# Linear attention with a SoLU block: three small sums by token placed later, and one transposition of queries done in two halves

## The chip, the cores and the metric

The kernel runs on one core of a Trainium2 chip. A core has five engines that run side by side, each with its own queue, in order: TensorE (PE; its weight loads are shown apart as PEld), VectorE (DVE), ScalarE (ACT), GpSimd (POOL) and SyncE (SP, which here issues DMAs). They wait for each other through semaphores. The metric is the time of one execution on the device in microseconds (us); the lower the better.

## What is computed

Attention with a recurrent state, then a feed-forward block on its output:

```python
for t in range(S):                                   # B, H, S, D = 4, 8, 768, 48
    state = alpha[:, :, t, :, None] * state + k[:, :, t] (outer) v[:, :, t]
    y[:, :, t] = q[:, :, t] @ state
x = y.transpose(0, 2, 1, 3).reshape(B * S, H * D)    # 3072 x 384
h = x @ w_in                                         # 3072 x 1024
e = exp(h - max(h)); solu = h * e / sum(e)
ln = (solu - mean) / sqrt(var + 1e-6) * g_ln
out = ln @ w_out                                     # 3072 x 384
```

## The kernel before

**Groups and chunks.** The sequence is cut into G = 6 groups of P = 128 tokens. A group holds the 128 tokens of all B = 4 batches, so there are 24 chunks of 128 tokens, numbered `n = g * 4 + b`. Queries, keys and alphas lie with 32 partitions for each batch. The head dimension of 48 is split in a first part of 32 (the "firsts", 8 heads of 32 x 128) and a last part of 16 (the "lasts", two heads in one block, 4 blocks).

**One group of attention.** Alpha is transposed (`alpha_T`, L179 and L182 on DVE), scanned backwards and forwards (`scan_back`, `scan_on`, L204 on DVE) into running products; keys and queries are multiplied by these. `lasts(qn, qe)` and `firsts(qn, qv)` are DVE transpositions in blocks of 32 x 32 (L182 and L179); `queries(2)` then multiplies the lasts, `queries(0)` the first four heads of the firsts and `queries(1)` the other four, each one POOL instruction of 128 x 512 (L253). `apart` (L245, two ACT instructions) spreads the lasts over the even and the odd heads. `move_lasts` (8 DMAs) and `move_firsts` (4 DMAs) copy the queries into `lot` for the reading of the state. `scores(a, half)` (L278 on PE) does four heads of the scores: first with the firsts of heads 0, 2, 1, 3, then with the lasts of the even heads and of the odd heads, for all four batches, into the PSUM banks a0 to a3. `masked(half)` (L289 on DVE) takes them out under the causal mask. `read_state` and `read_values` (L333) give y, and `next_state` (L371) the state of the next group.

**One group of the feed-forward block.** For each of the eight slices f of 128 features, `up` computes h (L394 on PE), e = exp(h) (L408 on ACT), u = h * e (L409 on DVE) and the square of u (L412 on ACT). `running` adds up e on POOL and the squares on DVE (both L427) over the slices. `token_sums` reduces these sums over the partitions with PE (L462), transposes the result on DVE (L467) and makes from it, for each token, `s`, the part of the variance that is independent of the mean (L469, L471, L473: three DVE instructions of 128 x 4 or 128 x 8). `down` multiplies by w_out (L507 on PE), whose extra column gives the sum of u, and `finish(n)` makes mean and variance from it (L532 to L537 on DVE, which reads `s`), takes the power -1/2 on POOL (L546), scales on ACT (L548) and stores.

**The order.** The program is written under a manual schedule: the order of the calls in the source is the order in each engine's queue. Waits between engines are put in from the reads and writes of regions of a tile. The first groups are written out by hand (to L845 or so): group 0 alone, then `token_sums(0)`, the preparation of group 1's attention beside the `down` of group 0, then `scores(1, 0)`, `masked(0)`, `alpha_T(2)`, `scores(1, 1)`, `masked(1)`, `finish(0)`, `finish(1)`, `finish(2)`. The group 0 sums' `token_sums(0)` stands ahead of `alpha_T(1)`; its result is first read in `finish(0)`.

From then on a loop over g runs the feed-forward of group g and the attention of group g + 1 together. In slice s of group g it issues in turn: what the plan has at "head", `up(g, s)`, a `finish`, `token_sums(g - 1)` at s = 0, what the plan has "behind", the `centre` steps in group 1, `running(g, s)`, what stands in the "middle", a `down`, and the "tail". For g = 1 the plan is

```python
first = dict(
    head={3: "keys_back"},
    behind={0: "v", 1: "on1", 2: "lasts firsts", 3: "apart", 4: "scores0 masked0", ...},
```

so `attend(2, "lasts")` and `attend(2, "firsts")` stand behind slice 2, ahead of `running(1, 2)`; `apart` behind slice 3, after that slice's square on ACT; and the first scores of the third group (a = 2) behind slice 4. For g = 2 to 4 the plan `usual` has "lasts firsts" at slice 2 too, for a = 3 to 5.

Of the kernel before, what the change touches and what calls it, by code (L numbers as in the profile page):

```python
# [9 lines left out]
FP = mybir.dt.float32  # L10
# [4 lines left out]
ALU = mybir.AluOpType  # L15
AX = mybir.AxisListType
P = 128
# [15 lines left out]
def fast_path(ctx, tc, q, k, v, alpha, moe_w_in, moe_w_out, moe_g_ln, out):  # L33
# [12 lines left out]
    nc = tc.nc  # L46
    B, H, S, D = q.shape
    NTOK, DM = out.shape
    DFF = moe_w_in.shape[1]
    G = S // P  # L50
    N = B * G
    NP = H // 2
# [9 lines left out]
    def pool(name, bufs, **kw):  # L62
        return ctx.enter_context(tc.tile_pool(name=name, bufs=bufs, **kw))
# [4 lines left out]
    small = pool("small", 4)  # L68
# [31 lines left out]
    qn = const.tile([P, H, TQ, D], FP, name="qn")  # L100
# [20 lines left out]
    qv = const.tile([P, 2 * H, SW], FP, name="qv")  # L121
# [6 lines left out]
    gr = [dict() for _ in range(G)]  # L128
# [44 lines left out]
    def load_v(g):  # L173
        t = slice(g * P, (g + 1) * P)
        for b in range(B):
            nc.sync.dma_start(out=held(vn, b), in_=v[b, :, t, :].rearrange("h p d -> p h d"))

    def firsts(src, dst):
        nc.vector.transpose(out=dst.rearrange("p h (t u) -> p h u t", u=TQ), in_=src[:, :, :, 0:E0])  # L179
# [31 lines left out]
    def inverses(g):  # L211
        nc.gpsimd.tensor_copy(out=fend[:, g], in_=h4[:, :, 1])  # L212
        nc.vector.reciprocal(out=seed[:, :, 0:1], in_=h4[:, :, 1:2])
# [5 lines left out]
    def keys_T(g):  # L219
        firsts(kn, kT[:, 0:H])  # L220
        lasts(kn, kT[:, H:NB])

    def keys(g):
        for part in (slice(0, H), slice(H, NB)):
            nc.gpsimd.tensor_tensor(out=kT[:, part], in0=kT[:, part], in1=hk[:, part], op=ALU.mult)  # L225
# [24 lines left out]
    def queries(i):  # L250
        part = slice(NP * i, NP * i + NP)
        q = qe[:, :, 0:P] if i == 2 else qv[:, part, 0:P]
        nc.gpsimd.tensor_tensor(out=q, in0=q, in1=aT[:, part, 1:SW], op=ALU.mult)  # L253
# [11 lines left out]
    def quarter(b):  # L265
        return slice(32 * b, 32 * b + 32)
# [4 lines left out]
    def scores(g, half, a=None):  # L271
        a = a or banks("a", [NP, P])
        for last in range(2):
            for i in (0, 2, 1, 3):
                h = half * NP + i
                kb, qb = (H + h // 2, H + h) if last else (h, h)
                for b in range(B):
                    nc.tensor.matmul(  # L278
                        a[b][:, i], lhsT=kT[quarter(b), kb], rhs=qv[quarter(b), qb, 0:P], start=not last and not i, stop=bool(last),
                        tile_position=(32 * b, 0), skip_group_check=True,  # L280
                    )
        masks[half] = a
# [3 lines left out]
    def masked(half, batches=range(B)):  # L286
        a = masks[half]
        for b in batches:
            nc.vector.tensor_tensor(  # L289
                out=sT[:, b, half * NP : half * NP + NP], in0=a[b], in1=mask[:, None, :].to_broadcast([P, NP, P]),  # L290
                op=ALU.mult,
            )
# [46 lines left out]
    def read_begin():  # L339
        reading["y"] = {}  # L340
        reading["begun"] = set()
# [112 lines left out]
    def token_sums(g):  # L454


        d = gr[g]
        t = ps_a.tile([P, B, 2, 32], FP, tag="a3", name="rows") if g else ps_h.tile([P, B, 2, 32], FP, tag="h", name="rows")
        for b in range(B):
            for r in range(4):  # L460
                c = b * P + 32 * r
                nc.tensor.matmul(  # L462
                    t[quarter(r), b], lhsT=d["unit"][:, 0:32], rhs=d["p"][:, :, c : c + 32], start=True, stop=True,
                    tile_position=(0, 32 * r), skip_group_check=True,
                )
        tt = work.tile([P, B, 2, 32], FP, name="cols")
        nc.vector.transpose(out=tt.rearrange("p b i t -> p (b i t)"), in_=t.rearrange("p b i t -> p (b i t)"))  # L467
        s = sums[:, g * B : g * B + B]
        nc.vector.tensor_copy(out=s[:, :, 1:3], in_=tt[:, :, :, 0])  # L469
        sq = small.tile([P, B], FP, name="sq")  # L470
        nc.vector.tensor_tensor(out=sq, in0=s[:, :, 1], in1=s[:, :, 1], op=ALU.mult)  # L471
        d["s"] = small.tile([P, B], FP, name="s")
        nc.vector.scalar_tensor_tensor(  # L473
            out=d["s"], in0=sq, scalar=1e-6 * DFF, in1=s[:, :, 2], op0=ALU.mult, op1=ALU.add
        )

    def last_norm():

# [39 lines left out]
    def finish(n):  # L518
        g, b = divmod(n, B)
        d = st[n]  # L520
        s, whole = sums[:, n], d.get("held", d["o"])
        o = whole[:, 0:DM]
        t0 = b * S + g * P
        if g == G - 1:
            o_sb = work.tile([P, DM], FP, name="o_sb")
            r = gr[g]["r"][:, b : b + 1]
            nc.vector.tensor_scalar(out=o_sb[:, 0:P], in0=o[:, 0:P], scalar1=r, scalar2=None, op0=ALU.mult)  # L527
            nc.scalar.activation(out=o_sb[:, P:DM], in_=o[:, P:DM], func=AF.Copy, scale=r)  # L528
            nc.scalar.dma_start(out=out[t0 : t0 + P, :], in_=o_sb)
            d.clear()  # L530
            return
        nc.vector.tensor_copy(out=s[:, 0:1], in_=whole[:, DM : DM + 1])  # L532
        t = small.tile([P, 1], FP, name="t")
        nc.vector.scalar_tensor_tensor(
            out=t, in0=s[:, 0:1], scalar=-1.0 / DFF, in1=s[:, 0:1], op0=ALU.mult, op1=ALU.mult
        )
        nc.vector.tensor_tensor(out=s[:, 3:4], in0=t, in1=gr[g]["s"][:, b : b + 1], op=ALU.add)  # L537
        if g == 0:

            centred = work.tile([P, DM], FP, name="o_mean")  # L540
            nc.vector.scalar_tensor_tensor(
                out=centred, in0=mean_sb, scalar=s[:, 0:1], in1=o, op0=ALU.mult, op1=ALU.add
            )
            o = centred
        r = small.tile([P, 1], FP, name="r")
        nc.gpsimd.tensor_tensor(out=r, in0=s[:, 3:4], in1=mhalf, op=ALU.pow)  # L546
        o_sb = work.tile([P, DM], FP, name="o_sb")
        nc.scalar.activation(out=o_sb, in_=o, func=AF.Copy, scale=r)  # L548
        nc.sync.dma_start(out=out[t0 : t0 + P, :], in_=o_sb)
        d.clear()  # L550
# [166 lines left out]
    for i in (0, 2, 1):  # L717
        if i == 1:
# [3 lines left out]
            out=qe[:, :, 0:P] if i == 2 else qv[:, part, 0:P], in0=t[i], in1=aT[:, part, 1:SW], op=ALU.mult  # L722
# [98 lines left out]
    down(2, 1)  # L821
    scores(1, 1)
    masked(1)
    finish(0)
    finish(1)
    finish(2)
# [36 lines left out]
    def attend(a, what):  # L863

        more = a + 1 < G
        if what == "v":
            load_v(a)
        elif what == "keys":
            keys_T(a)
            keys(a)  # L870
            if more:
                load(k, kn, a + 1)
        elif what[:2] == "on":
            if what == "on2":
                inverses(a)
            scan_on(a, int(what[2]))
        elif what == "lasts":
            lasts(qn, qe[:, :, 0:P])
            ends_of_decay()
            queries(2)  # L880
            move_lasts()
        elif what == "firsts":
            firsts(qn, qv[:, 0:H, 0:P])
            queries(0)
            queries(1)
            move_firsts()
            if more:
                load(q, qn, a + 1)
        elif what == "apart":
            apart()  # L890
        elif what == "decay":
            decay(a)
        elif what == "keys_back":
            if more:
                keys_back(a)
        elif what[:6] == "scores":
            scores(a, int(what[6]))
        elif what[:6] == "masked":
            masked(int(what[6]))
        elif what == "alpha" and more:  # L900
            alpha_T(a + 1)
            if a > 2:
                attend(a, "over")
        elif what == "over" and more:
            alpha_over(a + 1)
            if a + 2 < G:
                load(alpha, an, a + 2)
        elif what == "back" and more:
            for i in range(3):
                scan_back(a + 1, i)  # L910
        elif what == "begin":
            read_begin()
        elif what[:4] == "read":
            read_state(int(what[4]))
        elif what == "values":
            read_values(a)
        elif what == "kv" and more and a != 4:
            next_state(a)
# [3 lines left out]
    for g in range(1, G + 1):  # L922
# [10 lines left out]
        for s in range(FC):  # L933
# [18 lines left out]
            if todo:  # L952
                n, half = todo.pop(0)
# [24 lines left out]
    def compare(out, x, bound, op):  # L978
# [6 lines left out]
        out=chunks[:, :, 2], in0=sums[:, :, 2], scalar=0.25, in1=sums[:, :, 3], op0=ALU.mult, op1=ALU.is_le  # L985
# [6 lines left out]
    else:  # L992
# [9 lines left out]
        out=bad, in0=all_ok[0:1, 0:1], scalar1=float(P * ends[-1]), scalar2=None, op0=ALU.is_lt  # L1002
# [451 lines left out]
```

## Time and profile before

| | us |
|---|---|
| median of 3 runs (368.16 to 368.46) | 368.23 |
| the profiled execution, on the device | 367.97 |
| its span, first to last instruction | 366.2 |
| PE busy | 357.8 (98%) |
| PE weight loads busy | 215.0 (59%) |
| DVE busy | 245.0 (67%) |
| ACT busy | 146.4 (40%) |
| POOL busy | 132.2 (36%) |

The granted TensorE clock is 1.000 over the span. A profile is of one execution; times in it run from its first instruction. A timeline row gives start, length, engine, line, operation, output<-inputs by the program's names, shapes, the number of instructions merged, and in brackets the engine's idle time before it with the instruction that ended it. Ends of matmuls are modelled, since they are pipelined; start times are not. Neighbouring rows of DVE may overlap by about 0.1 us[...].

### The profile page before, as it was taken

Reading aid. Unit: us, or ns where it says so; the run is one execution under the profiler, and the core shown is the slowest. Engines: PE = TensorE matmul, PEld = TensorE weight load, DVE = VectorE, ACT = ScalarE, POOL = GpSimd, SP = SyncE. Lnnn points to the kernel's source line nnn. Section 1 sums busy time; section 2 is a strip of 40 time slices with the busy share of each in tenths; the row PEclk is TensorE's granted clock in tenths of the full one; section 3 lists DMA queues with packets and bytes.
Section 4 is the critical chain, followed back from the end, with each engine's and each line's share of the span. In section 5 each row is a group of like instructions: output and inputs, shape, how many; then the busy total and the mean of one; then the engine's idle time right before and its main releaser. Section 6 shows DMA issues by size and latency. Waiting matters only on the chain. (4 is left out here: it accounts for less than half of the span.)

```text
span 366.2 us, 10036 instructions
## 1 busy us (share of the span) xinstructions
PE 357.8 (98%) x4341; PEld 215.0 (59%) x4341; DVE 245.0 (67%) x375; ACT 146.4 (40%) x260; POOL 132.2 (36%) x129
## 2 busy tenths in 40 slices
PE   8899999999999999999999999999999999999994
PEld 8784355666755566566575456475556565555552
DVE  0999989979998797936675935766946314345420
ACT  3647878182645262252521252431241132222110
POOL 7020000004449963774133764232773121233300
PEclk9999999999999999999999999999999999999999
DMA  9995995326196409463035354004041000000011
GB/s 180 183 338 152 204 309 124 88 67 159 50 234 141 109 21 180 85 152 94 21 92 112 83 121 126 3 25 88 21 107 55 0 25 0 24 21 22 23 47 51
DMA packets 72871, 36.06 MB, mean 98 GB/s; under 512 B 48232, under 2 KB 70000, under 8 KB 72816
## 3 DMA queue, kind: packets, MB, share of 16 engines
q1 hardware_dynamic: 71792, 34.39, 39.8%
q10 hardware_dynamic: 1024, 0.92, 0.8%
q8 instruction: 36, 0.59, 0.7%
q14 instruction: 19, 0.16, 0.2%
HBM read 25.30 MB, written 4.72 MB: 82 GB/s over the span
## 5 line engine op out<-in xcount | busy, mean ns | idle before, releaser
L507 PE MATMUL o<-w_out,room 128*128 128x385 f32 x384 | 134.0, 492 | 0.0
L394 PE MATMUL h<-x,w_in 128*128 128x512 f32 x288 | 131.7, 597 | 0.5 <-DVE g_col L642 0.5
L507 PEld LDWEIGHTS o<-w_out,room 128*128 128x128 f32 x384 | 71.0, 189 | 54.7 <-issue 13.1
L394 PEld LDWEIGHTS h<-x,w_in 128*128 128x128 f32 x288 | 53.2, 189 | 58.6 <-issue 48.5
L409 DVE TENSOR_TENSOR room<-h,e 128x512 f32<-128x512 f32 x40 | 27.5, 689 | 72.9 <-ACT e L408 72.9
L408 ACT ACTIVATE e<-h 128x512 f32<-128x512 f32 x40 | 24.0, 599 | 100.2 <-PE h L394 100.2
L427 POOL TENSOR_TENSOR p<-p,e 128x512 f32<-128x512 f32 x30 | 43.7, 1458 | 20.0 <-ACT e L408 19.9
L412 ACT ACTIVATE u<-room 128x512 f32<-128x512 f32 x40 | 25.2, 630 | 38.3 <-DVE room L409 38.3
L546 POOL TENSOR_TENSOR r<-sums,mhalf 128x1 f32<-128x1 f32 x20 | 14.8, 741 | 69.7 <-DVE sums L537 69.4
L289 DVE TENSOR_TENSOR sT<-a,mask 128x512 f32<-128x512 f32 x43 | 26.7, 681 | 8.0 <-PE a L278 7.9
L204 DVE TENSOR_TENSOR_SCAN hT<-aT,unit 128x516 f32<-128x516 f32 x18 | 24.4, 1399 | 7.6 <-ACT aT L703 7.5
L204 DVE TENSOR_TENSOR_SCAN aT<-aT,seed 128x516 f32<-128x516 f32 x18 | 27.4, 1551 | 0.2
L225 POOL TENSOR_TENSOR kT<-kT,hT 128x1024 f32<-128x1024 f32 (+1 forms) x8 | 14.2, 1800 | 32.7 <-DVE kT L179 32.7
L427 DVE TENSOR_TENSOR p<-p,u 128x512 f32<-128x512 f32 x30 | 22.5, 749 | 5.1 <-ACT u L412 5.1
L278 PEld LDWEIGHTS a<-qv,kT 32*128 32x128 f32 x704 | 21.4, 186 | 7.0 <-issue 2.6
L278 PE MATMUL a<-qv,kT 32*128 32x128 f32 x704 | 23.9, 278 | 0.4 <-POOL qv L253 0.3
L212 POOL COPY fend<-hT 128x12 f32<-128x12 f32 x6 | 3.1, 509 | 55.9 <-DVE hT L204 55.9
L333 PE MATMUL y<-sT,vn 128*32 128x128 f32 x768 | 22.6, 273 | 0.2 <-DVE sT L289 0.2
L333 PEld LDWEIGHTS y<-sT,vn 128*32 128x32 f32 x768 | 20.7, 110 | 1.6 <-issue 1.0
L196 ACT ACTIVATE sq<-an,mone 128x1536 uint8<-128x1536 f32 x12 | 18.9, 1572 | 0.2
L548 ACT ACTIVATE o_sb<-o,r 128x384 f32<-128x384 f32 x16 | 9.3, 582 | 18.5 <-POOL r L546 18.5
L261 POOL TENSOR_TENSOR state<-state,lot 128x384 f32<-128x384 f32 x10 | 8.8, 903 | 13.1 <-DMA lot<-qv 13.1
(148 smaller groups left out, 374.3 us busy)
## 6 DMA issues: line engine op xcount, KB each, us to landing
vn<-in_v_dram SPq DMA_DIRECT2D x24, 192.0 KB, 4.7
an<-in_alpha_dram SPq DMA_DIRECT2D x20, 192.0 KB, 4.1
out_dram<-o_sb SPq DMA_DIRECT2D x20, 192.0 KB, 1.9
room<-in_moe_w_out_dram SPq DMA_DIRECT2D x8, 384.0 KB, 5.5
kn<-in_k_dram SPq DMA_DIRECT2D x16, 192.0 KB, 5.6
qn<-in_q_dram SPq DMA_DIRECT2D x16, 192.0 KB, 4.1
lot<-qe SPq DMA_DIRECT2D x40, 64.5 KB, 2.1
lot<-qv SPq DMA_DIRECT2D x20, 129.0 KB, 2.4
```

Of the source, the lines that this page charges most:

```text
L196: nc.scalar.activation(out=sq, in_=x, func=AF.Relu, scale=sign, bias=mone, accum_out=over[:, g, i : i + 1])
L204: nc.vector.tensor_tensor_scan(out=o, data0=a, data1=s, initial=1.0, op0=ALU.mult, op1=ALU.add)
L278: nc.tensor.matmul(a[b][:, i], lhsT=kT[quarter(b), kb], rhs=qv[quarter(b), qb, 0:P], start=not last and not i, stop=bool(last), tile_posit ...
L289: nc.vector.tensor_tensor(out=sT[:, b, half * NP : half * NP + NP], in0=a[b], in1=mask[:, None, :].to_broadcast([P, NP, P]), op=ALU.mult,)
L333: nc.tensor.matmul(y_bank(b)[quarter(r), a], lhsT=lhsT, rhs=rhs, start=(b, r) not in begun, stop=stop, tile_position=(row, 32 * r), skip_g ...
L394: nc.tensor.matmul(h, lhsT=w_in[:, a, f * P : (f + 1) * P], rhs=d["x"][:, a].rearrange("p b t -> p (b t)"), start=(a == 0), stop=(a == KC ...
L408: nc.scalar.activation(out=e, in_=h, func=AF.Exp)
L409: nc.vector.tensor_tensor(out=u, in0=h, in1=e, op=ALU.mult)
L412: nc.scalar.activation(out=u2, in_=u, func=AF.Square)
L427: eng.tensor_tensor(out=p, in0=d[0][i] if f == 1 else p, in1=d[f][i], op=ALU.add)
L507: nc.tensor.matmul(d["o"][:, 0 : DM + 1], lhsT=u_of(g, f)[:, b * P : b * P + P], rhs=w_out[:, f], start=(f == 0), stop=(f == FC - 1), skip ...
L546: nc.gpsimd.tensor_tensor(out=r, in0=s[:, 3:4], in1=mhalf, op=ALU.pow)
```

## The change

Two edits. In `token_sums` the three DVE instructions behind the transposition L467 become an inner function: for g > 0 it is called where they stood, for g = 0 it is kept and called ahead of `finish(0)`, after `masked(1)`. In `attend`, for a = 2, the transposition of the firsts is done in two parts of four heads, with the POOL product of each part issued after it; for other a it stays whole (`for j in range(0, 2)` then issues the same two products as before). NP is 4, H is 8.

```diff
         tt = work.tile([P, B, 2, 32], FP, name="cols")
         nc.vector.transpose(out=tt.rearrange("p b i t -> p (b i t)"), in_=t.rearrange("p b i t -> p (b i t)"))
         s = sums[:, g * B : g * B + B]
-        nc.vector.tensor_copy(out=s[:, :, 1:3], in_=tt[:, :, :, 0])
-        sq = small.tile([P, B], FP, name="sq")
-        nc.vector.tensor_tensor(out=sq, in0=s[:, :, 1], in1=s[:, :, 1], op=ALU.mult)
-        d["s"] = small.tile([P, B], FP, name="s")
-        nc.vector.scalar_tensor_tensor(
-            out=d["s"], in0=sq, scalar=1e-6 * DFF, in1=s[:, :, 2], op0=ALU.mult, op1=ALU.add
-        )
+        def rest():
+            nc.vector.tensor_copy(out=s[:, :, 1:3], in_=tt[:, :, :, 0])
+            sq = small.tile([P, B], FP, name="sq")
+            nc.vector.tensor_tensor(out=sq, in0=s[:, :, 1], in1=s[:, :, 1], op=ALU.mult)
+            d["s"] = small.tile([P, B], FP, name="s")
+            nc.vector.scalar_tensor_tensor(
+                out=d["s"], in0=sq, scalar=1e-6 * DFF, in1=s[:, :, 2], op0=ALU.mult, op1=ALU.add
+            )
+
+        if g:
+            rest()
+        else:
+            d["rest"] = rest
...
     scores(1, 1)
     masked(1)
+    gr[0]["rest"]()
     finish(0)
     finish(1)
     finish(2)
...
         elif what == "firsts":
-            firsts(qn, qv[:, 0:H, 0:P])
-            queries(0)
-            queries(1)
+            for i, n in ((0, NP), (NP, NP)) if a == 2 else ((0, H),):
+                firsts(qn[:, i : i + n], qv[:, i : i + n, 0:P])
+                for j in range(i // NP, (i + n) // NP):
+                    queries(j)
             move_firsts()
             if more:
                 load(q, qn, a + 1)
```

## The prediction

> **What bounds the kernel now.** I first read the busy shares on the page: TensorE (PE) is busy for 357.8 of the 366.2 us span, VectorE (DVE) for 245.0, ScalarE (ACT) 146.4, GpSimd (POOL) 132.2. The chain that ended last holds only the final output tile, so it says nothing about the middle. Since PE is nearly always busy, an edit on another engine can move the end only where PE waits for that engine. So I asked next for PE's waits between 58 and 135 us, where both edits lie. Columns: who waited, for whom, us in total, times, longest.
>
> ```profile
> PEld a L278 <- DVE qv L811: 0.3, 1, 0.3
> PE a L278 <- POOL qv L253: 0.3, 1, 0.3
> ```
>
> Both are scores (L278): one waits for DVE, one for POOL. The ends of matmuls are modelled, so a stall can hide inside a busy block. The PE timeline (start, length, what) shows it, because the same 64 matmuls recur:
>
> ```profile
> 77.87 2.69 PE L278 MATMUL a<-qv,kT 32*128 32x128 f32 x64
> ...
> 83.28 2.07 PE L278 MATMUL a<-qv,kT 32*128 32x128 f32 x64
> ...
> 107.55 5.32 PE L394 MATMUL h<-x,w_in 128*128 128x512 f32 x12
> 113.12 2.26 PE L278 MATMUL a<-qv,kT 32*128 32x128 f32 x64 [0.26 <-POOL qv L253]
> ```
>
> The undisturbed block is 2.07. The first one (group two, half 0) carries 0.62 of stall inside: bank a1 still holds the query block that L811 reads until 78.45. The one at 113.12 (group three, half 0) starts about 0.3 late (0.26 by modelled ends, 0.33 against the start-to-start step before the scores at 118.09) and has 0.19 inside. All of PE's stalls within reach are thus 0.62 + 0.33 + 0.19 = 1.14 us. After the block at 118.09, which is lengthened by 0.14 by the masking before it, equal blocks repeat at equal steps to 345 us: a shift of PE at 120 us is neither absorbed nor enlarged later, unless an engine falls behind.
>
> The DVE timeline next:
>
> ```profile
> 62.69 0.44 DVE L467 STREAM_TRANSPOSE cols<-rows 128x256 f32<-128x256 f32 x1
> 63.16 0.17 DVE L469 COPY sums<-cols 128x8 f32<-128x8 f32 x1
> 63.37 0.17 DVE L471 TENSOR_TENSOR sq<-sums 128x4 f32<-128x4 f32 x1
> 63.57 0.17 DVE L473 SCALAR_TENSOR_TENSOR s<-sq,sums 128x4 f32<-128x4 f32 x1
> 63.65 2.17 DVE L179 STREAM_TRANSPOSE aT<-an 128x1024 f32<-128x1024 f32 x1
> ...
> 109.55 2.05 DVE L179 STREAM_TRANSPOSE qv<-qn 128x1024 f32<-128x1024 f32 x1
> 111.43 0.69 DVE L427 TENSOR_TENSOR p<-p,u 128x512 f32<-128x512 f32 x1
> 112.02 0.69 DVE L409 TENSOR_TENSOR room<-h,e 128x512 f32<-128x512 f32 x1
> ...
> 118.12 1.50 DVE L427 TENSOR_TENSOR p<-p,u 128x512 f32<-128x512 f32 x1
> ```
>
> Here stand the three small sums that move, the transposition that is cut, and behind it the running sum L427 and the product L409. The same running sum takes 0.69 at 111.43 and 1.50 at 118.12. POOL says why:
>
> ```profile
> 109.78 1.09 POOL L253 TENSOR_TENSOR qe<-qe,aT 128x512 f32<-128x512 f32 x1 [1.65 <-DVE qe L182]
> 111.68 2.44 POOL L253 TENSOR_TENSOR qv<-qv,aT 128x512 f32<-128x512 f32 x2 [0.81 <-DVE qv L179]
> ...
> 117.11 1.96 POOL L662 TENSOR_TENSOR w_out<-w_out,mean_sb 128x384 f32<-128x384 f32 x2
> ```
>
> POOL's second L662 started at 118.07 and ended at 119.07; the DVE sum that came at 118.12 ended 0.55 later, at 119.61. It waited for the whole POOL instruction. Last, ACT:
>
> ```profile
> 112.75 0.63 ACT L412 ACTIVATE u<-room 128x512 f32<-128x512 f32 x1 [1.41 <-DVE room L409]
> 113.28 1.32 ACT L245 ACTIVATE qv<-qe,parity 128x512 f32<-128x512 f32 x2
> ```
>
> L245 (`apart`) makes the queries for the second halves of the score matmuls. It stands on ACT behind the square L412, which waits for DVE's L409. The odd heads' copy ends at 114.61 and PE starts their matmuls at 114.66. So this block of scores has two gates: POOL's first product at its start, and DVE -> ACT -> `apart` before its last quarter.
>
> **What the Trainium skill says.** "SBUF — State Buffer", section "Who interferes with whom": a DVE instruction with two SBUF inputs and a GpSimd instruction that reads SBUF exclude each other for the whole instruction, whichever issues first; a DVE instruction with one SBUF input does not contend. The trace agrees: the sum L427 was held at 118.12, while L253 took 1.09 beside the transposition, and L409, whose h lies in PSUM, keeps 0.69 beside POOL. "VectorE: DVE Perf Modes", section "The TRN2 errata — SBUF-src ops pay a fixed extra latency per instruction": small instructions cost mostly a fixed part. Here a 128x4 sum takes 0.17 and a 128x512 one 0.69.
>
> **Part 1, the sums by token.** Removed near 63 us: three instructions. From L467 to the next transposition is 0.97 now; L467 alone holds the engine for 0.3 to 0.4 (0.44 less the overlap of 0.08 to 0.15 seen between independent neighbours). DVE runs 0.6 to 0.65 earlier. It has no gap up to L811 at 77.76, apart from 0.1 ahead of L804, so bank a1 comes free at 77.85 and the 0.62 stall inside the first score block goes: PE gains 0.6. No other wait replaces it, since the matmuls ahead of it do not depend on this DVE work and the transposed keys in kT are ready at 72.5. The loads of alpha (SP at 66.87), `move_lasts` and `move_firsts` (SP at 74.78 and 80.15) come 0.6 earlier too, behind nothing new. The masks at 80.41, which wait for PE, follow by 0.6, and so does everything on DVE up to 88.02.
>
> Added ahead of `finish(0)`: copy to square 0.21, square to sum 0.20, sum to next 0.08, hence 0.49, with no POOL reader beside them. Queued behind: `finish(0..2)`, then `scan_back(2)` and all of DVE's work to 113 us. So from 88 us DVE is 0.6 - 0.49, about 0.12 early (0.05 to 0.2), while PE is 0.6 early. PE needs DVE in between only for the h buffers: L409 ends at 102.84 - 0.12, and the third h block wants its bank at 103.66 - 0.6 = 103.06. That holds. Alone, part 1 gains PE nothing lasting beyond this 0.12, since the scores of group three wait for DVE's descendants.
>
> **Part 2, the firsts in halves.** One 128x1024 transposition (1.88 to the next start) becomes two of 128x512. The nearest row is the lasts, 128x512, 0.96 to the next start at 109.55. Added: 0 to 0.06; below nothing is excluded, as the elements are the same. DVE's second half ends as before. With the 0.12 from part 1 the first half starts at 109.43 and lands at 110.54, POOL's product of the lasts (109.66 to 110.75) hides the wait, and `queries(0)` runs from 110.72 to 111.81 (1.09). Before, it ran from 111.68 to 113.07. PE's scores may start at 113.12 - 0.33 - 0.6 = 112.2 without a wait.
>
> But now DVE's L427 arrives at 111.43 - 0.12 to + 0.06, about 111.34, with `queries(0)` in the middle of its run. Both read two operands in SBUF. It is held to 111.81, and the next instruction, L409, starts 0.47 after POOL's end (119.07 to 119.54 in the example): 112.28 instead of 112.02, +0.26. Behind it in order: the square at 113.00 (0.72 later, as before), `apart` at 113.54 (0.54 later), its odd copy done at 114.86 (1.32 later), PE's odd quarter at 114.91 instead of 114.66. PE has meanwhile waited some 1.2 us in the middle of the block, where it now waits 0.19. So the start gate opens, and the other gate closes 0.25 later. Everything after on PE is 0.25 late.
>
> What else moves: `queries(1)` waits for L427 and ends near 113.45 instead of 114.12. `move_firsts` isn't helped, since SP is still issuing the eight `move_lasts` until 116.1. POOL's running sums come 0.5 to 0.7 earlier, and then meet DVE's L427 at 113.66 and at 118.37. The latter is nearly a tie with POOL's sum at 118.2: if POOL is first, L409 after it slips to 119.96 (0.42 later) and the masks free their last bank at 123.1, just before PE's `read_state` at 123.26. So no further PE loss, with 0.13 to spare; if DVE is first it recovers 0.4. From 127 us DVE idles 1.5 us and is level again.
>
> Sum: +0.25 on the profiled execution's 367.97 (span 366.2 and 1.8 around it), thus 368.2. The median of the runs is 0.26 above the profiled one, so I predict 368.23 + 0.25 = 368.5.
>
> **Rivals.**
> (a) DVE's L427 isn't held, for instance because it needs the port only briefly. Then `apart` keeps the 0.12 of part 1: 368.1. Against: three running sums (113.41, 118.12, 122.57) all end 0.55 after a POOL instruction.
> (b) Slower: POOL keeps the port from `queries(0)` straight into `queries(1)`, and L427 waits for both. Place: 111.8. Price: another 1.09 before L409, so `apart`, PE's odd quarter and the end are 1.3 late: 369.5. It decides if `queries(1)` starts right at 111.8. Against: at 119.03 POOL's next sum took 1.72, 0.45 more than its 1.27, so it let the waiting DVE in first. For it: all these handovers are POOL to DVE at other instructions. The same size would result if the second half's transposition had to wait for `queries(0)` to release `qv`. Against that, PE's first scores started at 113.12 while POOL was still writing the other heads.
> (c) Faster: all 1.14 us of stall go, 367.1. It needs `apart` about 1 us earlier, and nothing in the change moves it by more than 0.12. It would take a DVE start before 109 us that this trace does not show.
>
> **Chances.** Forecast 0.62, (a) 0.14, (b) 0.17, (c) 0.07. Within 0.2% is within 0.74 us, about what a measurement of this kernel can tell from no change. The forecast (0.05 of it beyond the bound, should the tie at 118.4 or the bank at 123.1 go wrong by half a microsecond) and (a) lie inside: same 0.71; slower 0.17 + 0.05 = 0.22; faster 0.07. The forecast's own range is 368.2 to 368.9, by the 0.05 to 0.2 of DVE's lead and that tie; to leave out no more than 2 in 10 the range takes in (a) and the lower part of (b): 367.9 to 369.5.
>
> **What would show it.** Right: the first score block near 77.9 back to about 2.07; L427 near 111.3 taking about 1.0 instead of 0.69; the block of the third group's first scores starting near 112.2 but ending near 115.6, with PE's wait now on ACT's L245. Wrong: an L427 of 0.69 there (a), of over 2 (b), or an `apart` that starts before 113 (c).

## The result, and the profile after

The changed kernel takes 368.62 us (median of 22 runs, 368.33 to 369.65) against 368.15 us for the kernel before (22 runs beside them, 367.66 to 369.10): ratio 1.0014, 95% interval 1.0009 to 1.0020, which is 0.3 to 0.7 us more. The profiled execution took 368.34 us with a span of 366.5, 0.37 us more than that of before.

PE's timeline of the changed kernel, the blocks that answer to those of before:

```profile
77.90 2.07 PE L278 MATMUL a<-qv,kT 32*128 32x128 f32 x64
...
112.19 1.17 PE L278 MATMUL a<-qv,kT 32*128 32x128 f32 x32
114.40 1.34 PE L278 MATMUL a<-qv,kT 32*128 32x128 f32 x32 [1.04 <-ACT qv L245]
```

The first score block has lost its 0.62 us of stall (2.07, the undisturbed length), and PE reaches the third group's first scores at 112.19, 0.93 earlier than before. It does the half of the block that uses the firsts, and then waits: what ends the wait is no longer POOL but ACT's `apart`. The next block starts at 115.67 instead of 115.32. From there to the end the PE blocks start 0.33 to 0.37 later than before, and the profiled execution is 0.37 longer: in the profile the loss is made here.

DVE and POOL of the changed kernel at that place:

```profile
109.55 2.09 DVE L179 STREAM_TRANSPOSE qv<-qn 128x512 f32<-128x512 f32 x2
111.49 0.97 DVE L427 TENSOR_TENSOR p<-p,u 128x512 f32<-128x512 f32 x1
112.39 0.68 DVE L409 TENSOR_TENSOR room<-h,e 128x512 f32<-128x512 f32 x1
...
118.47 1.55 DVE L427 TENSOR_TENSOR p<-p,u 128x512 f32<-128x512 f32 x1
119.95 0.68 DVE L409 TENSOR_TENSOR room<-h,e 128x512 f32<-128x512 f32 x1
```

```profile
109.78 1.09 POOL L253 TENSOR_TENSOR qe<-qe,aT 128x512 f32<-128x512 f32 x1 [1.66 <-DVE qe L182]
110.83 2.58 POOL L253 TENSOR_TENSOR qv<-qv,aT 128x512 f32<-128x512 f32 x2
```

POOL's `queries(0)` now starts at 110.83 instead of 111.68 and ends at 111.92. DVE's running sum L427, which had run ahead of it before, arrives at 111.49 in the middle of it, takes 0.97 instead of 0.69 and ends 0.55 after POOL. L409 behind it starts at 112.39, 0.37 later than before. ACT follows:

```profile
113.11 0.63 ACT L412 ACTIVATE u<-room 128x512 f32<-128x512 f32 x1 [1.76 <-DVE room L409]
113.64 1.32 ACT L245 ACTIVATE qv<-qe,parity 128x512 f32<-128x512 f32 x2
```

The square and `apart` start 0.36 late, and PE's block behind these scores 0.35.

Where the small sums went, on DVE:

```profile
79.98 2.48 DVE L289 TENSOR_TENSOR sT<-a,mask 128x512 f32<-128x512 f32 x4 [2.46 <-PE a L278]
...
87.63 0.14 DVE L470 COPY sums<-cols 128x8 f32<-128x8 f32 x1
87.81 0.17 DVE L472 TENSOR_TENSOR sq<-sums 128x4 f32<-128x4 f32 x1
88.01 0.17 DVE L474 SCALAR_TENSOR_TENSOR s<-sq,sums 128x4 f32<-128x4 f32 x1
88.09 0.15 DVE L538 COPY sums<-lot 128x1 f32<-128x1 f32 x1
```

The masks start at 79.98, 0.43 earlier than before; `finish(0)` starts at 88.09, 0.07 later. By the firsts DVE stands where it stood: 109.55 in both kernels.

### The profile page after: what moved, and what is told of

Read it like the earlier page. It is cut to its first block, busy times and chain, and to the rows that moved or that the text cites. A ratio compares the mean times of both kernels' runs of the same rounds, so it can differ in the third digit from the quotient of the medians.

```text
span 366.5 us, 10037 instructions
## 1 busy us (share of the span) xinstructions
PE 357.7 (98%) x4341; PEld 214.6 (59%) x4341; DVE 245.4 (67%) x376; ACT 146.2 (40%) x260; POOL 130.7 (36%) x129
## 5 line engine op out<-in xcount | busy, mean ns | idle before, releaser
L409 DVE TENSOR_TENSOR room<-h,e 128x512 f32<-128x512 f32 x40 | 27.5, 688 | 72.7 <-ACT e L408 72.7
L427 POOL TENSOR_TENSOR p<-p,e 128x512 f32<-128x512 f32 x30 | 42.1, 1405 | 20.0 <-ACT e L408 19.9
L427 DVE TENSOR_TENSOR p<-p,u 128x512 f32<-128x512 f32 x30 | 23.5, 782 | 5.2 <-ACT u L412 5.2
```

What stands on the lines that cost most here:

```text
L409: nc.vector.tensor_tensor(out=u, in0=h, in1=e, op=ALU.mult)
L427: eng.tensor_tensor(out=p, in0=d[0][i] if f == 1 else p, in1=d[f][i], op=ALU.add)
```

## The experiments

Timed ratios here have intervals of about +-0.1%, or +-0.35 us, as wide as the effects. So the readings rest on distances inside the traces, one profile of each kernel, and the ratios stand beside them. The traces also start differently: PE reaches the sums by token (L462 in the kernel before) at 60.18 us in the profile of before, at 60.21 after, and between 60.18 and 60.84 over all profiles, so the two that are compared above are among the earliest. A distance from one instruction to another is free of that, as long as the two hang together. "Firsts to scores" is the time from the start of the third group's transposition of firsts to the end of its first scores, read as the start of PE's next block, since ends of matmuls are modelled.

| kernel | first scores start | firsts start | firsts to scores | ratio to before (95%) |
|---|---|---|---|---|
| before | 77.87 | 109.55 | 5.77 | |
| after | 77.90 | 109.55 | 6.12 | 1.0014 (1.0009 to 1.0020) |
| e1 sums alone | 77.97 | 109.62 | 5.82 | 1.0012 (1.0001 to 1.0022) |
| e12 e1 again | 78.25 | 109.90 | 5.76 | 1.0005 (0.9996 to 1.0013) |
| e2 halves alone | 78.40 | 109.77 | 6.12 | 1.0001 (0.9993 to 1.0009) |
| e3 other half first | 78.08 | 109.72 | 5.77 | 1.0003 (0.9995 to 1.0012) |
| e4 sum behind product | 78.53 | 110.18 | 5.24 | 1.0006 (0.9993 to 1.0018) |
| e5 before, PE late | 78.31 | 109.53 | 5.75 | 1.0014 (1.0004 to 1.0024) |
| e6 sums alone, PE late | 78.41 | 110.06 | 5.83 | 1.0028 (1.0020 to 1.0035) |
| e7 spread early | 78.00 | 109.64 | 4.89 | 1.0002 (0.9992 to 1.0012) |
| e8 spread early, sums late | 78.23 | 109.96 | 4.77 | 1.0008 (1.0000 to 1.0016) |
| e9 new order | 78.27 | 109.90 | 4.80 | 0.9999 (0.9988 to 1.0010) |
| e10 new order alone | 78.19 | 109.73 | 5.44 | 0.9992 (0.9983 to 1.0001) |
| e11 e5 again | 78.77 | 109.95 | 5.76 | the profiled run alone |

**Each part alone.** My theory was that POOL's earlier product holds up DVE's sum and so `apart` (called "port"). The rivals: that the second transposition itself costs (cut), or that the sums at 88 us make DVE late (moved sums).

```diff
# e1: the whole change without the halves
-            for i, n in ((0, NP), (NP, NP)) if a == 2 else ((0, H),):
+            for i, n in ((0, H),):
# e2: the whole change without the moved sums
-        if g:
-            rest()
-        else:
-            d["rest"] = rest
+        rest()
...
-    gr[0]["rest"]()
```

> Only the three small sums are moved; the firsts are transposed whole. Theory (port): no change of the end, 0 +- 0.1 us against the kernel before. The first score block near 77.9 loses its 0.6 us of stall, PE arrives 0.6 early at the third group's first scores and waits there for POOL's queries(0) until 113.1, so about 0.9 us instead of 0.3; L427 behind the firsts takes 0.69. Rival (moved sums): the sums at 88 us make DVE late for all that follows, and this run alone is 0.3 us or more slower than before. Rival (cut): 0, since nothing is cut.

> Only the firsts of the third group are transposed in halves; the small sums stand where they stood. Theory (port): +0.37 us against before, as with the whole change: L427 near 111.5 takes about 1.0 us, L409 behind it starts at 112.4, and the block of first scores ends at 115.7. The first score block near 77.9 keeps its 0.6 us of stall. Rival (moved sums): 0. Rival (cut, the second transposition itself costs): +0.37 as well, so that this run does not tell it from the port.

The halves alone give the full 6.12 us, with L427 held. DVE of e2:

```profile
111.65 1.04 DVE L427 TENSOR_TENSOR p<-p,u 128x512 f32<-128x512 f32 x1
112.61 0.68 DVE L409 TENSOR_TENSOR room<-h,e 128x512 f32<-128x512 f32 x1
```

The moved sums alone (e1) give 5.82, and 5.76 in the second run of that kernel (e12), as before, with L427 at 0.74 and 0.68: no loss in this stretch. DVE and PE of e1:

```profile
111.50 0.74 DVE L427 TENSOR_TENSOR p<-p,u 128x512 f32<-128x512 f32 x1
```

```profile
113.24 2.26 PE L278 MATMUL a<-qv,kT 32*128 32x128 f32 x64 [0.30 <-POOL qv L253]
```

So the 0.35 that the traces lose in this stretch belongs to the halves. Two expectations missed. In e1 PE waited for POOL only 0.37 us, counted in start times, instead of 0.9: it had already lost 0.61 at 94.7 us in a wait that nothing shown ended, and that came out of the same wait; in e12 it is 0.94. And the timed runs don't order the two parts as the traces do. For e2 the interval is 0.3 us less to 0.3 us more than before, whose upper end only touches the 0.35 of its trace; for e1 it is 0 to 0.8 us more, with no loss in its trace. By the medians of the same runs (e1 368.32, e2 368.29, before 368.09) the two parts cost about the same. So the timed runs by themselves do not say which part makes the loss.

**The cut or the port.** This run keeps both transpositions but swaps them, so that `queries(0)` can't start before L427.

```diff
-            for i, n in ((0, NP), (NP, NP)) if a == 2 else ((0, H),):
+            for i, n in ((NP, NP), (0, NP)) if a == 2 else ((0, H),):
                 firsts(qn[:, i : i + n], qv[:, i : i + n, 0:P])
-                for j in range(i // NP, (i + n) // NP):
-                    queries(j)
+            queries(0)
+            queries(1)
```

> The whole change, but heads 4 to 7 are transposed before heads 0 to 3, and both products come after: as many DVE instructions as in the change, while queries(0) can start only after the second half, when L427 has begun. Theory (port): L427 takes 0.69 to 0.72, L409 starts at 112.0 to 112.1, the end is 0 +- 0.12 us against before, and PE waits for POOL until 113.1 to 113.2. Rival (cut): L409 stays at 112.3 to 112.4 and the end at +0.3. Rival (moved sums): +0.3.

DVE and PE of e3:

```profile
109.72 2.06 DVE L179 STREAM_TRANSPOSE qv<-qn 128x512 f32<-128x512 f32 x2
111.61 0.69 DVE L427 TENSOR_TENSOR p<-p,u 128x512 f32<-128x512 f32 x1
112.20 0.69 DVE L409 TENSOR_TENSOR room<-h,e 128x512 f32<-128x512 f32 x1
```

```profile
113.29 2.27 PE L278 MATMUL a<-qv,kT 32*128 32x128 f32 x64 [0.87 <-POOL qv L253]
```

As many DVE instructions, L427 back at 0.69, firsts to scores 5.77. From the firsts to L409 it is 2.48, as in the kernel before (2.47), against 2.84 with the change. The cut costs nothing that can be seen in this stretch; the loss is in the time at which POOL's product runs. Further on e3 loses 0.21 us that the kernel before doesn't: at `read_state`, from 123.18 to the next block at 124.48, 1.30 instead of 1.10, where PE's weight loads wait for POOL's state product. The kernel before with a late PE (e11, below), which has neither part of the change, loses as much at the same place, so this is not put down to the cut.

**The sum put behind the product.** Here the halves stay, and L427 is taken from in front of L409.

```diff
                 up(g, s)
+                if (g, s) == (1, 3):
+                    later.pop()()
```

`later` holds the call that issues DVE's running sum of slice 2.

> The whole change, but DVE's running sum of slice 2 is issued behind the product L409 of slice 3 instead of ahead of it, so that what POOL holds up isn't ahead of L409. Theory (port): L409 starts at 111.5 instead of 112.39, apart ends near 114.0, the third group's first scores end at 114.8 instead of 115.67; the end is between 0 and 0.2 us below the kernel before, since the second scores then wait for the masks, which stand behind two sums on DVE. Rival (cut, or moved sums): L409 gains no more than the 0.6 us of the sum itself against 112.39, hence 111.8 or later, and the end stays above that of the kernel before.

DVE and PE of e4:

```profile
110.18 2.11 DVE L179 STREAM_TRANSPOSE qv<-qn 128x512 f32<-128x512 f32 x2
112.05 0.77 DVE L409 TENSOR_TENSOR room<-h,e 128x512 f32<-128x512 f32 x1
```

```profile
113.09 2.39 PE L278 MATMUL a<-qv,kT 32*128 32x128 f32 x64
115.42 2.84 PE L394 MATMUL h<-x,w_in 128*128 128x512 f32 x6
118.19 2.80 PE L278 MATMUL a<-qv,kT 32*128 32x128 f32 x64
```

L409 follows the transposition by 1.87 us instead of 2.84, and firsts to scores falls to 5.24. The second scores then take 0.73 longer than the undisturbed 2.07, since they wait for the masks, which stand behind two sums on DVE. They end 10.74 us after the firsts' start, where the change has 11.03 and the kernel before 10.68. So the mechanism stands, and the small gain that I expected at the end didn't come.

**The second gate by itself.** `apart` is put ahead of slice 3's square on ACT (the third argument of `up_act` is called between product and square):

```diff
-        up_act(g, f)
+        up_act(g, f, apart if (g, f) == (1, 3) else None)
...
-            0: "v", 1: "on1", 2: "lasts firsts", 3: "apart", 4: "scores0 masked0", ...
+            0: "v", 1: "on1", 2: "lasts firsts", 4: "scores0 masked0", ...
```

> The whole change, with apart (L245, two ACT instructions) of the third group issued ahead of slice 3's square instead of behind it. L427 is still held. Theory (port, closing gate is apart behind the square): PE has no wait for ACT left, the third group's first scores run from 112.2 to 114.2 (2.0 us), and PE then waits 1 us or more for the masks in the second scores, which end no earlier than 0.1 us below the kernel before; the end is -0.2 to +0.2 us against before. Rival (the gate is another, such as POOL or DVE directly): the first scores still end after 115.

PE of e7:

```profile
112.53 2.07 PE L278 MATMUL a<-qv,kT 32*128 32x128 f32 x64
114.53 2.84 PE L394 MATMUL h<-x,w_in 128*128 128x512 f32 x6
117.30 3.14 PE L278 MATMUL a<-qv,kT 32*128 32x128 f32 x64
```

With L427 still held (1.10), the first scores have no wait: the gate that closed was `apart` behind the square. All of it is given back in the second scores, 3.14 instead of 2.07, which wait for DVE's masks. The second scores end 10.73 us after the firsts' start, against 10.68 before. So in this order PE's earlier arrival is worth nothing at the end, since DVE's masks come next.

**A late PE.** The timed loss is 0.47 us by the medians and the profiles' 0.37, which its interval of 0.3 to 0.7 still holds; but e1, which loses nothing in its trace, measured above 1. With the sums moved there is no wait left inside the first score block, and in the kernel before this wait could swallow a PE that comes late from the start. Two idle matmuls of 128x128 ahead of `down(1, 0)` make PE late at a fixed place:

```diff
+    warm(2, ps_a, "a1")
     down(1, 0)
     scaled(7)
```

> The kernel before, with two idle matmuls of 128x128 on PE ahead of the second chunk's down at 60.8 us; their result is not used. They make PE about 0.5 us late at a place that depends on nothing of DVE. Theory (cushion): in the kernel before such lateness is swallowed by the 0.62 us wait for bank a1 inside the first score block, which shrinks to about 0.1; the firsts of the third group start at the same distance from the alpha transposition at 63.6 as before (45.9 us), and the end is 0 to +0.15 us against before. Rival (no cushion): PE's 0.5 us stay to the end, +0.5.

> The moved sums alone, firsts whole, with the same two idle matmuls on PE. Theory (cushion): with the sums moved there is no wait left inside the first score block, so PE's 0.5 us reach the masks, DVE's sums at 88 us, the firsts and the third group's scores: about +0.5 us against before and +0.5 against the moved sums alone, and the firsts start at about 110.05 instead of 109.6. That would explain why the change measures more than the 0.37 us that its profile shows. Rival (no cushion effect): the end of this run is as that of the kernel before with the same two matmuls.

> The kernel before with two idle matmuls on PE once more, for its profile. In the first look PE's lateness was gone at the third group's scores, and 0.44 us were lost at 142 us in a wait that no semaphore ended. If that belongs to chance, it is not there now and the span from the second scores' end to the scores of the fourth group is 43.45 us as before; if it belongs to the program, it is there again and that distance is 43.9.

> The moved sums alone once more, for a narrower interval. Theory (cushion): a profile that begins as early as that of before shows no loss, but PE's later starts pass through, so the median is 0.1 to 0.3 us above before. Rival: no difference, within 0.1 us.

PE and DVE of e5, the kernel before with PE late:

```profile
78.31 2.07 PE L278 MATMUL a<-qv,kT 32*128 32x128 f32 x64
```

```profile
109.53 2.04 DVE L179 STREAM_TRANSPOSE qv<-qn 128x1024 f32<-128x1024 f32 x1
```

and of e6, the moved sums with PE late:

```profile
78.41 2.07 PE L278 MATMUL a<-qv,kT 32*128 32x128 f32 x64
```

```profile
110.06 2.12 DVE L179 STREAM_TRANSPOSE qv<-qn 128x1024 f32<-128x1024 f32 x1
```

PE is late by 0.44 and 0.54 against before. In e5 the stall in the score block shrinks to nothing and the firsts start on time; in e6 they are late by 0.51. (DVE came to the query block L812, L811 in the kernel before, at 77.44 in e5, 0.32 earlier than before, so that nothing of the stall was left where about 0.1 was expected.)

The two columns of the table say the same without any idle matmuls. In each kernel with moved sums the firsts are late by about what PE was late at the first scores: e12 +0.38 and +0.35, e9 +0.40 and +0.35, e8 +0.36 and +0.41, e4 +0.66 and +0.63. In e2 and e10, where the sums are not moved, PE was late by 0.53 and 0.32, and the firsts by 0.22 and 0.18, which is about what DVE was late at the small sums (63.16 before, 63.41 in e2, 63.35 in e10). In e11 PE was late by 0.90, more than the wait of 0.62 can swallow, and the firsts by 0.40. So the moved sums take away a cushion of up to 0.62 us.

In time, e6 is 0.7 to 1.3 us above before. But e5 is above it as well, by 0.1 to 0.9 us where 0 to 0.15 was expected. By the medians e6 is 0.58 us above e5 (369.27 of 22 runs, 368.69 of 13), while the moved sums without a late PE cost 0.23 (e1) and 0.20 (e12). This points to the cushion and against the rival that e6 ends as e5 does, though the step from 0.2 to 0.58 is about what such medians scatter. The trace of e5 is level with before at 120.2 us and then takes 44.00 us instead of 43.45 to the fourth group's first scores. Of these 0.55 us, 0.44 are lost ahead of 142.02 in a wait that nothing shown ended, and 0.10 in the block that follows. In the second profile of that kernel (e11) this distance is 43.82: 0.21 more for POOL's state at 123.4 us, and at 142 only the 0.10. It has further such waits at 240, 287 and 294 us, 0.76 together with that at 142. So neither of the two answers fits: the wait at 142 is not the program's at its first size, and others took its place. What they are is open.

The cushion is shown in the traces up to 120 us. How much of the timed 0.47 us its loss makes is not settled, since e12 measured +0.2 us with an interval that reaches no change.

**Towards a faster order.** With `apart` ahead of the square, I also moved DVE's running sums of group 1: first those of slices 2 and 3 behind `masked(0)` (e8), then the one of slice 2 behind slice 3's product and those of slices 3 and 4 behind `masked(1)` (e9), and the latter on the kernel before, with neither part of the change (e10).

```diff
+            if i and g == 1 and f in (2, 3, 4):
+                later.append(add)
+            else:
+                add()
...
+                up(g, s)
+                if (g, s) == (1, 3):
+                    later.pop(0)()
...
             at("behind", s)
+            while later and s == 5:
+                later.pop(0)()
```

This is e9's edit beside the one of `apart`, which is as in e7; `add` issues one engine's sum. e8 holds back slices 2 and 3 only, issues both at s == 4, and has nothing at slice 3.

> As the run before, and DVE's running sums of slices 2 and 3 are issued behind masked(0) in slice 4, so that neither stands ahead of L409 or of the masks. Theory (port, and DVE's order is what PE waits for): first scores 112.2 to 114.2, masks from about 114.4, second scores from 117.0 with at most 0.2 us of wait inside; PE is 1.0 to 1.2 us ahead of the kernel before, ratio about 0.997. Rival (PE gains are taken back later by POOL's state or by banks): the lead is below 0.4 us at the end.

> The whole change, with apart of the third group ahead of slice 3's square, DVE's running sum of slice 2 behind the product of slice 3, and those of slices 3 and 4 behind masked(1). Theory: with neither a held sum nor apart in front, the first scores run 112.2 to 114.2 and the second 117.0 to 119.0 without a wait, masked(1) ends by 122.2, and PE reaches read_state at about 121.9; there it waits for POOL's state product, which waits for the last of the DMAs of move_firsts (121.2 us on SP's queue, not moved by any of this), until 122.9. So of 1.1 us won some 0.9 are taken back there: -0.1 to -0.3 us against before. Rival (no such gate): the full 1.1 us stay, ratio about 0.997.

> The kernel before with the three moves of the run above, without the moved small sums and without the halves. Theory: PE arrives at the third group's first scores at 112.8, queries(0) is ready at about the same time, so 0.5 us are won up to 120 us and the state of POOL takes back all but 0.1 of it: -0.1 us against before, and not slower than the run above, since the wait in the first score block that swallows a late PE is kept. Rival (halves or moved sums are needed): no gain ahead of 120 us, PE's first scores still at 113.1.

In all three both score blocks take 2.07 without a wait, here in e10:

```profile
113.18 2.07 PE L278 MATMUL a<-qv,kT 32*128 32x128 f32 x64
...
117.95 2.07 PE L278 MATMUL a<-qv,kT 32*128 32x128 f32 x64
```

e8 measured 1.0008, where about 0.997 was expected. Its gain was lost at `read_state`: three sums stood ahead of `masked(1)`, and PE waited for the banks that it frees (2.54 us to the next block instead of 1.10):

```profile
123.36 1.52 PE L333 MATMUL y<-lot,state 64*32 64x128 f32 x62 [0.69 <-DVE sT L289]
```

In e9 PE waited there for POOL, but for a reason of its own:

```profile
121.27 2.09 POOL L261 TENSOR_TENSOR state<-state,lot 128x384 f32<-128x384 f32 x2 [1.76 <-DMA lot<-qv]
```

Two state products take 1.65 in the kernel before and 2.09 here, and the second of them 1.29 instead of 0.85: DVE's sum at 121.96, which took 0.70, was running when it was issued. It is the same meeting as in the change, with the sides reversed. In e10 the sum comes at 122.43, the products take 1.64, and the expected wait at `read_state` isn't there: PE starts 0.32 later than in the profile of before and is 0.27 ahead of it at the fourth group's scores (163.41 against 163.68). Its median is 368.00 against 368.22 beside it. It is the best of all kernels here, but the interval reaches 1, so that it beats the kernel before is likely and not shown.

## Why the prediction was right

The forecast of 368.5 us, no change that clears 0.2%, stands against 368.62 and +0.14%. The number alone says little: the range of 367.9 to 369.5 us also held no change at all and alternative (a). What decides is the path that the forecast named, which the profile follows: an L427 of about 1.0, first scores that start near 112.2 and end near 115.6, and PE waiting on L245. By its steps:

- **The stall in the first score block goes.** Shown: 2.07, and from the start of L467 to the next transposition's 0.36 instead of 0.96.
- **DVE would be 0.12 early from 88 us on.** This term was wrong by its own size or more: 0.07 late at 88 us, level at 109.55. The sums cost 0.46, about as worked out. The masks were 0.43 early instead of 0.6. The first mask needs bank a0 alone, and in the kernel before this bank seems to have run ahead of the other three while they waited: there PE's last row of matmuls holds three starts (80.28 to 80.29) with the fourth one a row earlier (80.17); after, all four stand together (79.68 to 79.70). Which bank is missing from the last row is inferred, as the names in the trace don't tell banks apart. If so, this explains 0.11 of the 0.17; the rest is smaller differences.
- **The cut costs 0 to 0.06.** e3 shows 0.01 from the firsts to L409 (2.48 against 2.47).
- **L427 is held by `queries(0)`.** Shown: 0.97 at 111.49 (1.0 near 111.3 was forecast), and back to 0.69 in e3. The end came 0.55 after POOL's, as in the examples of before. Alternative (a), that it isn't held, falls; so does (b), that POOL keeps the port for its next product: that product took 1.54 and let DVE in first. It is as "SBUF — State Buffer", section "Who interferes with whom", of the Trainium skill has it: two SBUF inputs on DVE and a reading GpSimd instruction exclude each other. L409, with one operand in PSUM, kept 0.68.
- **L409 at 112.28, `apart` at 113.54, PE's next block at 115.57 (115.32 + 0.25).** Measured 112.39, 113.64, 115.67: each 0.1 late by the missing lead. So +0.36 in the profiles instead of +0.25.
- **The near tie at 118.4.** POOL came first (118.20 against 118.47), the L409 behind it started at 119.95 (119.96 was forecast), and PE lost nothing more.
- **Alternative (c), all stalls go.** Its condition, an `apart` about 1 us earlier, was more than met in e7 (111.28 instead of 113.28), and even that gained nothing: the masks were next. The prediction stopped one gate short there.

What it did not have: that the stall removed by part 1 was also what swallowed a late PE. It expected the whole loss from part 2 and a gain of 0.12 us from part 1. The traces bear out the loss of part 2, though 0.36 instead of 0.25, and not the gain. The timed runs bear out neither: they give the halves alone 0.3 us less to 0.3 us more, and the moved sums alone 0 to 0.8 us more in e1 and 0.1 less to 0.5 more in e12. That the median came within 0.12 us of the forecast is therefore in part luck.

## What to carry to other kernels

A stall is worth removing only with the gate behind it: ask which wait ends last in the same block, and then in the next one. When an instruction on GpSimd is released earlier, look at which two-operand instruction of VectorE it will now meet, and what is queued behind that. A wait in front of a common resource can be a cushion for a start that varies; the profile of one execution in which that start is early doesn't show it.

## What the runs showed of the hardware

In the meetings shown here the exclusion of DVE and POOL works both ways and goes by turns: a 128x512 product on POOL took 1.54 instead of 1.09 behind a waiting DVE sum, a DVE sum 0.97 instead of 0.69, and the two state products together 2.09 instead of 1.65. I had not expected one of the four banks that a round of matmuls writes to run ahead of the others while these wait, as the starts at 80.17 and at 80.28 to 80.29 suggest. And PE sometimes waits for nothing that the trace shows: 0.61 us in e1 at 94.7, 0.44 in e5 at 142, four times 0.1 to 0.3 in e11.
